# Batch 0's scores taken key tile by key tile over both kv pairs, with the value and sum matmuls of two query tiles split into single key tiles

## The chip, the cores and the metric

The kernel runs on one core of one Trainium2 chip. The metric is the device time of one execution in microseconds (us); the time before is the median of six runs. The engines are named as the profile names them: PE (TensorE, the matmul engine; PEld is its weight load), DVE (VectorE), ACT (ScalarE), POOL (GpSimd) and SP (SyncE, which here only issues DMAs).

## The reference

Grouped-query attention is followed by a gated MLP with a spatial gate, for eight batches:

```python
# attention: q (8, 16, 384, 64), k and v (8, 4, 384, 64); 4 query heads share one kv head
scores = matmul(q, k^T) / sqrt(64)
attn   = exp(scores - max) / sum(exp(scores - max))
x      = matmul(attn, v)                       # heads side by side: (8, 384, 1024)
# gated MLP
h      = relu(x @ w_in)                        # 1024 -> 1024
u, v   = h[..., :512], h[..., 512:]
v_n    = (v - mean(v)) / sqrt(var(v) + 1e-6)
v_s    = w_spatial @ v_n + b_spatial           # over the 384 positions
out    = (u * v_s) @ w_out                     # 512 -> 1024
```

## The kernel before, in words

**The work of one batch.** The 384 positions are three tiles of 128. A score unit is one query tile (`qt`), one pair of kv heads (`gp`, 0 or 1) and one key tile (`t`): `score_mm` (L363) makes a 128x1024 tile of scores with two matmuls that each use 64 rows of the PE array, and `exp` (L377) turns it into the fp16 tile `aT` on ACT. There are 18 units in a batch; the units go by query tile, then pair, then key tile. Two PSUM tiles hold scores (`ps_sc`, two buffers, L149), so a score unit can be computed when the exponential two units back is done.

`value_mm` (L388, matmuls on L395) multiplies `aT` with v, 32 columns at a time: `part` 0 and 1 are the two halves of the head dimension, `part` 2 multiplies with ones and so gives the sums of the softmax. One call is 12 matmuls over three key tiles and four kv heads, and it accumulates in one PSUM bank. The reciprocal of the sums comes from ACT as a logarithm and an exponential (`rec_ln`, `rec_exp`) or, for the first query tile of batch 0 alone, from DVE (`rec_v`, L414); `xmul` (L420) multiplies on DVE and leaves x transposed in `xt`.

The MLP follows: `v_mm` (steps V) or its halves (`v_part`, L595) for the v half of `h`, `relu`, `stats`, `rstd` and `norm` for `v_n`, `sp_part` for the spatial product (tile `psp`), `u_part` for the u half (`pu`), `sp_add` and `gate` on DVE, `o_part` for the output product (`po`), `o_copy` and `store`. The `..._part` functions use half of the array's rows and are paired, one on the low rows and one on the high rows. Between the two phases of such a pair stands a `mark` (L691): a tiny memset on DVE or POOL that waits for the end of phase 0 and that phase 1 waits for.

**What sets the order.** The order of every instruction on every engine is written out by hand in three plans, run by `run` (L729): `FIRST` for batches 0 to 2, `STEADY` once for each of batches 3 to 6, and `LAST` for batch 7. A step is a name, a batch (relative in `STEADY` and `LAST`) and arguments. The steps that matter here:

- `S`, `E`: the next score unit, the next exponential; `X,b,qt,part`: a value product; `rv`, `rl`, `re`: reciprocals; `xm`: `xmul`.
- `lk`, `lq`, `lv`, `lwi`, `lwo`, `lws`: loads of k, q, v, w_in, w_out, w_spatial. `lwi` goes out on POOL's queue and the first q tile of pair 0 on ACT's, all others on SP's.
- `ck`, `cq`, `cv`, `cws`, `cwo`: casts to fp16, with the engine as last letter (`v` DVE, `s` ACT, `p` POOL). `Tk`, `Tq`, `Tw`: transposes on PE; `tk`, `tq`, `tw`: the copies of their results. For batches from 2 on, `dk` and `dq` transpose by DMA instead.
- `V`, `ru`, `bs`, `rs`, `nm`: v half, relu, statistics, rstd, norm. `G`: a part of a paired product (`gs` spatial, `gu` u half, `go` output, `w..` v half beside output), `mk`: its mark.
- `W,0,n`: n warm-up matmuls of the identity with itself, whose result nobody reads.

Each engine runs its own steps in the order of the plan and waits only for its data and its buffers. Results other than scores go to four further PSUM banks, handed out in the order in which they were last read (`bank`, `read`, L168 and L174).

**The head of the kernel.** Before batch 0's first score, k and q are loaded, cast and transposed on PE. Batch 0's pair 0 is loaded first; the plan begins with 33 warm-up matmuls, then `Tk` and `Tq` of pair 0. Score units 0 to 2 need pair 0 alone, units 3 to 5 pair 1. The first `X` stands behind score unit 8.

Of the kernel before, what the change touches and what calls it, by code (L numbers as in the profile page):

```python
# [10 lines left out]
FP32 = mybir.dt.float32  # L11
# [7 lines left out]
SPLIT = 0  # L19

FIRST = """
lk,0,0,2 W,0,2 W,0,4 W,0,2 W,0,4 lq,0,0,0,1,0,1,s cq,0,0,0,1,1,0,1,p W,0,4 W,0,4 W,0,2 W,0,4 W,0,4
ck,0,0,0,3,s W,0,2 W,0,1 lq,0,1,0,1 cq,0,0,0,1,0,0,1,v Tk,0,0,0,3 Tq,0,0,0,0,1 lk,0,2,4
tq,0,0,0,0,1,v lq,0,0,1,3 tk,0,0,0,3,s lq,0,1,1,3 ck,0,1,0,3,p lk,1 lv,0 cq,0,1,0,1,1,0,1,p
cq,0,1,0,1,0,0,1,p lwi,0,1,2 lwi,0,1,1 lv,1 lwi,0,1,3 W,0,3 W,0,2 cq,0,1,1,3,1,0,1,p S,0 W,0,4 S,0
W,0,1 lq,1,0 Tk,0,1,0,3 Tq,0,1,0,0,1 S,0 W,0,1 E,0 lq,1,1 E,0 tk,0,1,0,3,v tq,0,1,0,0,1,v S,0 lws,0
lk,2 W,0,2 lwi,0,1,0 ck,1,0,0,3,p ck,1,1,0,3,p cv,0,p S,0 W,0,4 cq,0,0,1,3,0,0,1,v
cq,0,0,1,3,1,0,1,v lbi,0 lq,2,0 Tq,0,0,1,0,1 S,0 Tq,0,0,2,0,1 cq,1,0,0,1,0,0,1,p cq,0,1,1,3,0,0,1,v
tq,0,0,1,0,1,v S,0 Tq,0,1,1,0,1 W,0,1 Tq,0,1,2,0,1 E,0 lq,2,1 S,0 Tk,1,0,0,3 E,0 tq,0,0,2,0,1,v E,0
tk,1,0,0,3,v E,0 tq,0,1,1,0,1,v tq,0,1,2,0,1,v S,0 E,0 X,0,0,2 S,0 E,0 E,0 S,0 X,0,0,0 E,0 lwi,0,0,0  # L30
cq,1,1,0,1,0,0,1,p E,0 S,0 X,0,0,1 S,0 E,0 X,0,1,2 rv,0,0 xm,0,0,0 xm,0,0,1 lwi,0,0,3
cq,1,0,1,3,0,0,1,p S,0 X,0,1,1 X,0,1,0 cq,1,0,1,3,1,0,1,p E,0 S,0 rl,0,1 S,0 V,0,0,0,4 E,0 re,0,1
xm,0,1,1 V,0,0,4,8 S,0 xm,0,1,0 cv,1,v E,0 cws,0,0 lwi,0,0,1 cq,1,1,1,3,1,0,1,p cws,0,2 cws,0,1 E,0
lwi,0,0,2 cq,1,1,1,3,0,0,1,p S,0 cq,1,0,0,1,1,0,1,v ru,0,0,v V,0,1,0,4 Tq,1,0,0,0,1 Tk,1,1,0,3 E,0
E,0 tq,1,0,0,0,1,v bs,0,0 tk,1,1,0,3,s X,0,2,2 S,0 S,0 V,0,1,4,8 cq,1,1,0,1,1,0,1,v
cq,2,0,0,3,1,0,1,p cq,2,0,0,3,0,0,1,p Tq,1,1,0,0,1 tq,1,1,0,0,1,v rl,0,2 E,0 re,0,2 E,0 X,0,2,0
cq,2,1,0,3,0,0,1,p cq,2,1,0,3,1,0,1,p X,0,2,1 S,0 S,0 xm,0,2,0 xm,0,2,1 ru,0,1,v Tq,1,0,1,0,1
V,0,2,0,4 Tq,1,0,2,0,1 Tw,0,2,3 S,0 E,0 tq,1,0,2,0,1,v S,0 E,0 tw,0,2,3 bs,0,1 tq,1,0,1,0,1,v
ck,2,1,0,3,v ck,2,0,0,3,s E,0 V,0,2,4,8 Tw,0,0,2 Tq,1,1,1,0,1 E,0 tq,1,1,1,0,1,s ru,0,2,v tw,0,0,2
bs,0,2 X,1,0,2 S,0 rl,1,0 X,1,0,0 X,1,0,1 Tq,1,1,2,0,1 S,0 re,1,0 xm,1,0,0 S,0 E,0 xm,1,0,1 rs,0  # L40
dk,2 lwo,0,0 E,0 nm,0,2 nm,0,1 tq,1,1,2,0,1,v dq,2,0 lwo,0,1 nm,0,0 E,0 dq,2,1 lwo,0,2 lwo,0,3
V,1,0,0,4 V,1,0,4,8 S,0 ru,1,0,v G,0,gs,2,0,0,1 S,0 mk,0,gs,2,v E,0 G,0,gs,0,0,0,1 G,0,gs,2,1,0,1
S,0 mk,0,gs,0,v E,0 G,0,gs,0,1,0,1 E,0 S,0 sa,0,2 sa,0,3 sa,0,1 sa,0,0 X,1,1,2 E,0 rl,1,1 lk,3
X,1,1,0 X,1,1,1 lv,2 lq,3,0 lq,3,1 S,0 re,1,1 G,0,gu,2,0,0 S,0 G,0,gu,2,0,1 E,0 S,0 xm,1,1,1
xm,1,1,0 G,0,gu,0,0,0 E,0 E,0 cwo,0,0,1,v cwo,0,1,1,v S,0 G,0,gu,0,0,1 cwo,0,0,0,p mk,0,gu,2,p S,0
G,0,gu,2,1,0 mk,0,gu,0,p S,0 G,0,gu,0,1,0 E,0 G,0,gu,0,1,1 S,0 G,0,gu,2,1,1 gt,0,0 gt,0,3 gt,0,2 E,0
S,0 X,1,2,1 X,1,2,2 E,0 cwo,0,1,0,p E,0 S,0 cwo,0,2,1,v gt,0,1 cwo,0,2,0,v S,0 V,1,1,0,4 V,1,1,4,8
cwo,0,3,1,p E,0 rl,1,2 E,0 E,0 cwo,0,3,0,s re,1,2 G,0,go,0,0,0 ru,1,1,v S,0 xm,1,2,1 S,0 E,0
G,0,go,0,0,1 E,0 X,1,2,0 mk,0,go,0,p G,0,go,0,1,0 xm,1,2,0 bs,1,0 ck,3,0,0,3,v S,0 E,0 G,0,go,0,1,1
oc,0,0,v cv,2,p cq,3,0,0,3,1,0,1,p ck,3,1,0,3,p oc,0,1,s cq,3,0,0,3,0,0,1,v S,0 cq,3,1,0,3,0,0,1,p  # L50
cq,3,1,0,3,1,0,1,p X,2,0,2 X,2,0,0 S,0 rl,2,0 E,0 G,1,w12,2,0,0 G,1,w12,2,0,1 E,0 re,2,0 S,0 S,0
mk,1,w12,2,v bs,1,1 xm,2,0,0 G,1,w12,2,1,0 E,0 oc,0,2,v E,0 G,1,w12,2,1,1 S,0 ru,1,2,s oc,0,3,s
X,2,1,2 bs,1,2 X,2,0,1 rl,2,1 X,2,1,1 X,2,1,0 S,0 xm,2,0,1 re,2,1 xm,2,1,1 E,0 rs,1 G,2,w24,0,0,0
S,0 nm,1,0 xm,2,1,0 nm,1,2 G,2,w24,0,0,1 S,0 E,0 mk,2,w24,0,v nm,1,1 G,2,w24,0,1,0 S,0 E,0 oc,0,4,v
E,0 G,2,w24,0,1,1 E,0 ru,2,0,s lq,4,0 dk,3 lv,3 dq,3,0 dq,3,1 G,1,gs,0,0,0,1 S,0 oc,0,5,v
mk,1,gs,0,v S,0 G,1,gs,0,1,0,1 sa,1,0 E,0 G,1,gs,2,0,0,1 mk,1,gs,2,v sa,1,1 S,0 G,1,gs,2,1,0,1
G,1,gu,0,0,0 sa,1,3 sa,1,2 S,0 G,1,gu,0,0,1 mk,1,gu,0,v E,0 S,0 G,1,gu,2,0,0 G,1,gu,2,0,1
G,1,gu,0,1,0 S,0 E,0 E,0 mk,1,gu,2,v G,1,gu,0,1,1 S,0 G,1,gu,2,1,0 gt,1,0 S,0 G,1,gu,2,1,1 X,2,2,2
E,0 gt,1,1 bs,2,0 E,0 X,2,2,0 S,0 E,0 E,0 rl,2,2 re,2,2 E,0 gt,1,3 gt,1,2 G,2,w10,1,0,0
G,2,w10,1,0,1 mk,2,w10,1,v xm,2,2,0 S,0 S,0 G,2,w10,1,1,0 E,0 G,2,w10,1,1,1 E,0 S,0 st,0,1 lv,4 lk,4  # L60
X,2,2,1 oc,1,0,v oc,1,1,v ru,2,1,s bs,2,1 xm,2,2,1 cv,3,p st,0,2 lq,4,1 st,0,0 st,1,0 E,0
"""

STEADY = """
ck,1,0,0,3,p ck,1,1,0,3,p X,0,0,2 rl,0,0 X,0,0,0 S,0 G,-1,w12,2,0,0 G,-1,w12,2,0,1 re,0,0 S,0 S,0
E,0 E,0 cv,1,p cq,1,0,0,3,1,0,1,p cq,1,1,0,3,1,0,1,p cq,1,0,0,3,0,0,1,p xm,0,0,0 mk,-1,w12,2,v
cq,1,1,0,3,0,0,1,s G,-1,w12,2,1,0 G,-1,w12,2,1,1 oc,-2,3,s dq,1,0 oc,-2,2,s dk,1 S,0 lv,2 st,-2,1
dq,1,1 lk,2 ru,-1,2,v X,0,1,2 lq,2,1 lq,2,0 X,0,0,1 X,0,1,0 X,0,1,1 bs,-1,2 xm,0,0,1 rl,0,1 re,0,1
rs,-1 E,0 E,0 xm,0,1,0 G,0,w24,0,0,0 G,0,w24,0,0,1 nm,-1,1 nm,-1,0 xm,0,1,1 mk,0,w24,0,v nm,-1,2 S,0
S,0 E,0 G,0,w24,0,1,0 E,0 oc,-2,4,v G,0,w24,0,1,1 S,0 G,-1,gs,0,0,0,1 mk,-1,gs,0,p ru,0,0,s  # L70
oc,-2,5,v S,0 G,-1,gs,2,0,0,1 G,-1,gs,0,1,0,1 mk,-1,gs,2,p E,0 S,0 G,-1,gs,2,1,0,1 sa,-1,0 sa,-1,1
sa,-1,3 sa,-1,2 X,0,2,2 E,0 rl,0,2 X,0,2,0 X,0,2,1 re,0,2 E,0 S,0 G,-1,gu,0,0,0 G,-1,gu,0,0,1
mk,-1,gu,0,p xm,0,2,1 xm,0,2,0 E,0 G,-1,gu,2,0,0 S,0 G,-1,gu,0,1,0 G,-1,gu,2,0,1 S,0 S,0
G,-1,gu,0,1,1 mk,-1,gu,2,p G,-1,gu,2,1,0 E,0 E,0 G,-1,gu,2,1,1 E,0 S,0 gt,-1,0 gt,-1,1 gt,-1,2
gt,-1,3 S,0 G,0,w10,1,0,0 bs,0,0 G,0,w10,1,0,1 E,0 S,0 S,0 E,0 E,0 mk,0,w10,1,v E,0 G,0,w10,1,1,0
G,0,w10,1,1,1 S,0 ru,0,1,s oc,-1,0,v oc,-1,1,v st,-1,0 st,-2,2 bs,0,1 E,0
"""

LAST = """
S,0 X,0,0,2 G,-1,w12,2,0,0 G,-1,w12,2,0,1 E,0 rl,0,0 S,0 S,0 mk,-1,w12,2,v G,-1,w12,2,1,0  # L80
G,-1,w12,2,1,1 ru,-1,2,v oc,-2,3,v S,0 X,0,1,2 X,0,0,1 re,0,0 E,0 oc,-2,2,s rl,0,1 bs,-1,2 X,0,0,0
xm,0,0,1 xm,0,0,0 X,0,1,1 X,0,1,0 S,0 re,0,1 E,0 E,0 rs,-1 E,0 xm,0,1,1 G,0,w24,0,0,0 nm,-1,2
G,0,w24,0,0,1 mk,0,w24,0,v nm,-1,0 xm,0,1,0 S,0 S,0 G,0,w24,0,1,0 oc,-2,4,v G,0,w24,0,1,1 ru,0,0,v
E,0 E,0 X,0,2,2 oc,-2,5,s X,0,2,0 X,0,2,1 rl,0,2 V,0,1,0,4 bs,0,0 V,0,1,4,8 re,0,2 xm,0,2,1 nm,-1,1
ru,0,1,s xm,0,2,0 SP,-1,1 SP,-1,2 V,0,2,0,4 V,0,2,4,8 bs,0,1 sa,-1,1 U,-1,3 SP,-1,3 ru,0,2,v bs,0,2
sa,-1,2 rs,0 U,-1,1 SP,-1,0 U,0,0,1 nm,0,2 st,-2,1 sa,-1,3 U,-1,2 sa,-1,0 gt,-1,3 gt,-1,1 nm,0,1
U,-1,0 nm,0,0 st,-2,2 gt,-1,0 gt,-1,2 SP,0,1 SP,0,0 O,-1,0 sa,0,1 sa,0,0 oc,-1,0,v O,-1,5 SP,0,2
O,-1,3 O,-1,4 sa,0,2 oc,-1,4,s oc,-1,3,s oc,-1,5,s O,-1,1 SP,0,3 U,0,2 oc,-1,1,v gt,0,0 gt,0,2 U,0,1
gt,0,1 sa,0,3 O,-1,2 st,-1,2 U,0,3 gt,0,3 oc,-1,2,s O,0,1,0,3 O,0,4 O,0,1,3,4 O,0,0,0,3 oc,0,4,s
st,-1,0 st,-1,1 O,0,0,3,4 O,0,2 O,0,3 st,0,2,0,512 oc,0,0,v oc,0,1,s oc,0,2,v oc,0,3,s st,0,0  # L90
st,0,1,0,512 st,0,1,512,1024 lo,0,5
"""

# [2 lines left out]
def kernel(  # L96
# [20 lines left out]
    P = 128  # L117

    B, HQ, S, D = q.shape
# [5 lines left out]
    NST = S // P  # L125
# [234 lines left out]

    def score_mm(b, u, j0=0, js=1):  # L363
        qt, gp, t = u // 6, (u % 6) // 3, u % 3
        sc = ps_sc.tile([P, 2, 512], FP32, name=f"sc_{b}_{u}_{j0}", tag="sc")
        for half in range(2):
            lo, hi = half * D, (half + 1) * D
            nc.tensor.matmul(  # L368
                sc[:, half, 0 : 512 // js],
                kT[b][lo:hi, gp, t, :],  # L370
                qT[b, gp][lo:hi, qt, j0::js],
                start=True,
                stop=True,
            )
        held["sc", b, u, j0] = sc

    def exp(b, u, j0=0, js=1):  # L377
        qt, gp, t = u // 6, (u % 6) // 3, u % 3
        if (b, qt) not in aT:
            aT[b, qt] = att_a.tile([P, NGP, NST, 2, 512], FP16, name=f"aT_{b}_{qt}", tag="aT")  # L380
        nc.scalar.activation(  # L381
# [3 lines left out]
            scale=scale,  # L385
        )

    def value_mm(b, qt, part):  # L388

        a = aT[b, qt]  # L390
        v16 = loaded["v16", b]
        dst = bank([P, 512], FP32, f"X_{b}_{qt}_{part}")
        for t in range(NST):
            for g in range(HKV):
                nc.tensor.matmul(  # L395
                    dst[32 * g : 32 * (g + 1), :],
# [2 lines left out]
                    start=(t == 0),  # L399
                    stop=(t == NST - 1),  # L400
                )
        held["X", b, qt, part] = dst

    def rec_ln(b, qt):
        r = r_pool.tile([P, 512], FP32, name=f"rec_{b}_{qt}", tag="rec")
# [370 lines left out]
```

## Time and profile before

| | |
|---|---|
| median of six runs | 248.7 us (248.16 to 249.32) |
| the profiled execution, its own time | 249.3 us |
| its span, first to last instruction | 247.5 us |
| mean granted PE clock over the span | 0.997 |
| PE busy | 239.2 us, 97% |
| ACT busy | 190.7 us, 77% (139.9 us in exponentials) |
| DVE busy | 143.8 us, 58% |
| POOL busy | 42.8 us, 17% |

The profile shows one execution. "Busy" is the time in which at least one instruction of the engine runs; matmuls are pipelined, so that a busy PE says little by itself, and the distance from one matmul's start to the next is the better measure. In a line of the timeline the first two numbers are the start of a group of like instructions and the time from there to the end of the last one, both in us; a bracket at the end gives the idle time before and what ended it. A line of windows gives, for a stretch of time, each engine's busy time and its number of instructions.

### The profile page before, as it was taken

The page shows a single profiled execution, that of the slowest core. Times are in us where ns is not written, and L with a number is a line of the kernel's source. Part 1 is how long each engine was busy: PE and PEld are TensorE (multiplying, and loading weights), DVE is VectorE, ACT ScalarE, POOL GpSimd, SP SyncE. Part 2 cuts the span into 40 slices and gives each one's busy share as a digit, 9 for nine tenths or more (in the row PEclk, how much of TensorE's full clock was granted, in tenths as well). Part 3 has the DMA queues.
Part 4 walks back from the last instruction along what each step waited for, and adds up shares of the span by engine and source line. Part 5 has one row for each costly group of instructions (what it writes and reads, how often), then busy time and mean ns, then how long its engine had stood idle before and what let it go on. Part 6 is the DMA issues. An engine that isn't in the chain of part 4 may idle for free.

```text
span 247.5 us, 6053 instructions
## 1 busy us (share of the span) xinstructions
PE 239.2 (97%) x2556; PEld 120.5 (49%) x2556; DVE 143.8 (58%) x280; ACT 190.7 (77%) x249; POOL 42.8 (17%) x87
## 2 busy tenths in 40 slices
PE   7899998999999999999999999999999999999993
PEld 7434444543448444554445544554445544455551
DVE  0476698456774558636476447636476437777532
ACT  3899898999987888878997899888997797610221
POOL 1811914205015100033000600024000000000000
PEclk9999999999999999999999999999999999999998
DMA  7999999995999079910999049930950042200156
GB/s 175 293 219 343 245 216 196 273 320 162 263 322 276 3 172 199 300 45 12 260 243 285 4 171 223 299 108 3 265 151 0 3 165 91 85 2 1 41 223 247
DMA packets 57756, 42.73 MB, mean 173 GB/s; under 512 B 26881, under 2 KB 53889, under 8 KB 57729
## 3 DMA queue, kind: packets, MB, share of 16 engines
q1 hardware_dynamic: 54368, 39.85, 57.8%
q0 software_dynamic: 2176, 2.10, 5.6%
q10 hardware_dynamic: 1184, 0.39, 0.6%
q8 instruction: 20, 0.33, 0.5%
q14 instruction: 8, 0.06, 0.1%
HBM read 25.95 MB, written 12.58 MB: 156 GB/s over the span
## 4 chain that ended last, share of the span: by engine, by line
PE 84%; ACT 10%; DVE 3%; issue 1%; POOL 0%; POOLq 0%
PE X L395 18%; PE pu L613 13%; PE sc L368 11%; PE po L640 11%; PE pv L600 11%; ACT aT L381 7%; PE psp L626 4%; PE po L545 4%; PE pv L438 4%; PE pu L510 4%; PE warm L705 2%; DVE v_n L470 2%; PE psp L484 2%; DVE v_s L496 1%; ACT rec L412 1%
## 5 line engine op out<-in xcount | busy, mean ns | idle before, releaser
L381 ACT ACTIVATE aT<-sc 128x1024 f16<-128x1024 f32 x144 | 139.9, 1025 | 17.7 <-PE sc L368 17.7
L640 PE MATMUL po<-w_out,gT 64*128 64x512 f16 x288 | 66.9, 376 | 0.4 <-DVE mark_v L694 0.4
L600 PE MATMUL pv<-w_in,xt 64*128 64x512 f16 x272 | 64.5, 376 | 0.0
L368 PE MATMUL sc<-qT,kT 64*128 64x512 f16 x288 | 50.5, 380 | 1.3 <-ACT aT L381 1.3
L424 DVE TENSOR_TENSOR xt<-X,rec 128x512 f16<-128x512 f32 x48 | 32.0, 685 | 13.0 <-ACT rec L412 7.7
L395 PE MATMUL X<-aT,v 128*32 128x512 f16 x576 | 35.8, 380 | 0.0
L613 PE MATMUL pu<-xt,w_in 64*128 64x384 f16 x384 | 35.6, 322 | 0.0
L640 PEld LDWEIGHTS <-gT 64*128 64x128 f16 x288 | 25.7, 94 | 16.5 <-DVE mark_v L694 3.0
L600 PEld LDWEIGHTS <-xt 64*128 64x128 f16 x272 | 25.1, 94 | 15.9 <-issue 2.1
L522 DVE SCALAR_TENSOR_TENSOR gT<-pu,v_s 128x384 f16<-128x384 f32 x31 | 16.0, 552 | 22.7 <-PE pu L613 18.9
L328 DVE COPY osb<-po 128x512 f32<-128x512 f32 x28 | 19.3, 690 | 15.4 <-PE po L640 9.2
L368 PEld LDWEIGHTS <-kT 64*128 64x128 f16 x288 | 15.9, 94 | 23.1 <-issue 11.9
L613 PEld LDWEIGHTS <-w_in 64*128 64x128 f16 x384 | 20.5, 94 | 11.8
L328 POOL CAST q<-q 128x768 f16<-128x768 f32 (+2 forms) x29 | 21.0, 751 | 25.7 <-DMA q<-in_q_dram 20.5
L326 ACT ACTIVATE osb<-po 128x512 f32<-128x512 f32 x19 | 10.6, 595 | 18.1 <-PE po L545 17.4
L496 DVE TENSOR_TENSOR v_s<-psp,bias_b 128x384 f32<-128x384 f32 x32 | 20.3, 684 | 6.9 <-PE psp L626 6.3
L395 PEld LDWEIGHTS <-v 128*32 128x32 f16 x576 | 16.4, 96 | 14.4 <-issue 2.1
L395 PE MATMUL X<-aT,ones 128*32 128x512 f16 x288 | 20.1, 382 | 0.2
L696 POOL MEMSET mark_p<- 1x1 f32 x19 | 1.9, 102 | 104.8 <-PE psp L626 70.7
L406 ACT ACTIVATE rec<-X 128x512 f32<-128x512 f32 x23 | 13.8, 600 | 6.5 <-PE X L395 6.2
L459 DVE BATCH_NORM_STATS2 stats<-v_r 128x6 f32<-128x512 f32 x24 | 16.6, 690 | 3.0 <-issue 1.4
L449 DVE TENSOR_SCALAR v_r<-pv 128x512 f32<-128x512 f32 x12 | 8.2, 687 | 13.2 <-PE pv L600 10.7
(59 smaller groups left out, 204.3 us busy)
## 6 DMA issues: line engine op xcount, KB each, us to landing
out_dram<-osb SPq DMA_DIRECT2D x22, 512.0 KB, 3.7
q<-in_q_dram SPq DMA_DIRECT2D x14, 768.0 KB, 7.8
v<-in_v_dram SPq DMA_DIRECT2D x8, 384.0 KB, 4.9
k<-in_k_dram SPq DMA_DIRECT2D x7, 384.0 KB, 4.4
w_in<-in_moe_w_in_dram POOLq DMA_DIRECT2D x8, 256.0 KB, 7.4
w<-in_moe_w_out_dram SPq DMA_DIRECT2D x4, 512.0 KB, 4.5
q<-in_q_dram SPq DMA_DIRECT2D x2, 512.0 KB, 6.5
out_dram<-osb SPq DMA_DIRECT2D x3, 256.0 KB, 2.4
```

The source lines that it names most:

```text
L328: engine.tensor_copy(dst, src)
L368: nc.tensor.matmul(sc[:, half, 0 : 512 // js], kT[b][lo:hi, gp, t, :], qT[b, gp][lo:hi, qt, j0::js], start=True, stop=True,)
L381: nc.scalar.activation(aT[b, qt][:, gp, t].rearrange("p h (j q) -> p h j q", j=G)[:, :, j0::js], held["sc", b, u, j0][:, :, 0 : 512 // js] ...
L395: nc.tensor.matmul(dst[32 * g : 32 * (g + 1), :], v16[:, g, t, 32 * part : 32 * (part + 1)] if part < 2 else ones32, a[:, g // 2, t, g % 2 ...
L406: nc.scalar.activation(r, held["X", b, qt, 2], AF.Ln)
L424: nc.vector.tensor_tensor(xt[:, jj, :, qt * P : (qt + 1) * P], held["X", b, qt, jj].rearrange("p (j q) -> p j q", j=G), held["rec", b, qt] ...
L459: nc.vector.bn_stats(s6, held["v_r", b, st])
L496: nc.vector.tensor_tensor(held["v_s", b][:, m, :].rearrange("p (t s) -> p t s", t=NST), held["psp", b, m][:, 0:S].rearrange("p (t s) -> p ...
L522: nc.vector.scalar_tensor_tensor(held["gT", b][:, mu, :], held["pu", b, mu][:, 0:S], 0.0, held["v_s", b][:, mu, :], op0=ALU.max, op1=ALU.mult,
L600: yield lambda kc=kc: nc.tensor.matmul(held["pv", b, st], xT[b][rows, kc, st * P : (st + 1) * P], w_in16[rows, kc, DH:DFF], start=(first a ...
L613: yield lambda kc=kc: nc.tensor.matmul(held["pu", b, mu][:, 0:S], w_in16[rows, kc, mu * P : (mu + 1) * P], xT[b][rows, kc, :], start=(firs ...
L640: yield lambda m=m: nc.tensor.matmul(held["po", b, i], held["gT", b][rows, m, tt * P : (tt + 1) * P], w_out16[rows, m, half * 512 : (half ...
```

## The change

Two functions change, and all three plans are written anew.

In batch 0 the units go by query tile, then key tile, then pair: unit 1 is already pair 1. The other batches keep their order. `value_mm` takes a range of key tiles, so that a product can be made in pieces, with other work of PE between them:

```diff
+    def unit(b, u):
+        if b == 0:
+            return u // 6, u % 2, (u % 6) // 2
+        return u // 6, (u % 6) // 3, u % 3
...
-        qt, gp, t = u // 6, (u % 6) // 3, u % 3
+        qt, gp, t = unit(b, u)
...
-    def value_mm(b, qt, part):
+    def value_mm(b, qt, part, t0=0, t1=NST):
...
-        dst = bank([P, 512], FP32, f"X_{b}_{qt}_{part}")
-        for t in range(NST):
+        if t0 == 0:
+            held["X", b, qt, part] = bank([P, 512], FP32, f"X_{b}_{qt}_{part}")
+        dst = held["X", b, qt, part]
+        for t in range(t0, t1):
```

The plans, cut to PE's steps of the head (before, then after; the steps `W` ahead of the first `Tk` are 33 and 28 matmuls):

```diff
-Tk,0,0,0,3 Tq,0,0,0,0,1 W,0,3 W,0,2 S,0 W,0,4 S,0 W,0,1 Tk,0,1,0,3 Tq,0,1,0,0,1 S,0 W,0,1 S,0 W,0,2 S,0
-W,0,4 Tq,0,0,1,0,1 S,0 Tq,0,0,2,0,1 S,0 Tq,0,1,1,0,1 W,0,1 Tq,0,1,2,0,1 S,0 Tk,1,0,0,3 S,0 X,0,0,2 S,0 S,0
-X,0,0,0 S,0 X,0,0,1 S,0 X,0,1,2 S,0 X,0,1,1 X,0,1,0 S,0 S,0 V,0,0,0,4 V,0,0,4,8 S,0 S,0
+Tk,0,0,0,3 W,0,2 W,0,4 W,0,4 Tq,0,0,0,0,1 W,0,1 Tk,0,1,0,3 W,0,2 S,0 Tq,0,1,0,0,1 S,0 S,0 W,0,4
+Tq,0,0,2,0,1 S,0 S,0 Tq,0,0,1,0,1 W,0,2 X,0,0,2,0,1 S,0 X,0,0,2,1,2 Tq,0,1,1,0,1 S,0 X,0,0,1,0,1
+X,0,0,2,2,3 S,0 X,0,0,0,0,1 S,0 W,0,4 X,0,0,1,1,2 S,0 X,0,0,0,1,2 X,0,0,1,2,3 S,0 X,0,0,0,2,3 Tk,1,0,0,3
+S,0 Tk,1,1,0,3 Tq,0,1,2,0,1 S,0 X,0,1,1,0,1 X,0,1,1,1,2 X,0,1,0,0,1 S,0 X,0,1,2,0,1 X,0,1,0,1,2
+X,0,1,2,1,2 X,0,1,2,2,3 X,0,1,1,2,3 X,0,1,0,2,3 S,0 S,0 V,0,0,0,4 S,0 V,0,0,4,8 Tq,1,0,0,0,1 S,0
```

Query tiles 0 and 1 of batch 0 have their value products split; query tile 2 and all other batches keep whole ones. The number of warm-up matmuls in all (51), of score units and of all other PE instructions is the same before and after (2556 matmuls).

The rest of what moves, engine by engine:

- **Loads on SP.** Before: k pair 0, q pair 1 (its first query tile), k pair 1, then the rest of q, k of batch 1, v of batch 0, v of batch 1, q of batch 1. After: k pair 0, k pair 1, q pair 1, the rest of q, v of batch 0, k and q of batch 1, w_spatial, v of batch 1; the first two tiles of w_out are asked for earlier, the first one ahead of k and q of batch 2.
- **Casts at the start.** ACT casts half of pair 0's q, pair 1's k and half of pair 1's q, all ahead of its first exponential (before: pair 0's k, and a copy of its transpose). DVE casts pair 0's k and the other half of its q, POOL the other half of pair 1's q.
- **Batch 1's second product, around 65 to 75 us.** The mark of `w24` stood on DVE behind three `xmul`s and two of the three `norm`s; now it stands behind the same `xmul`s and one `norm`. On ACT an exponential stood between `re` and `rs`; now `rs` follows at once. The score units that stood singly between the halves of `w24` now stand in twos between its phases.
- **STEADY.** The marks of the spatial product and one of the two of the u half go from POOL to DVE; one relu goes from DVE to ACT and one from ACT to DVE; one of ACT's two output copies goes to DVE; ACT casts another half of q; loads and casts are in another order. PE keeps three blocks of whole value products in each pass.
- **LAST.** The spatial and u products of batch 6 and the norms of batch 7 are in another order; the last steps are the same kinds, and the plan ends with the same split output product (`lo`).

## The prediction

> **What bounds the kernel now.** I read the busy time by stages first, then PE, ACT and DVE in order of time. The stages:
>
> ```profile
> 6.40:14.00 7.60, 6.66 (x62) 3.68 (x63) 3.17 (x9) 6.91 (x8) 6.36 (x11) 1.00 1.17 274
> 14.00:20.50 6.50, 6.14 (x86) 1.98 (x85) 5.13 (x5) 6.50 (x9) 0.00 (x0) 1.00 1.17 255
> 20.50:39.50 19.00, 18.22 (x174) 8.12 (x172) 15.30 (x30) 17.45 (x25) 9.36 (x15) 1.00 1.04 251
> 39.50:100.40 60.90, 60.40 (x700) 29.90 (x702) 36.20 (x75) 54.59 (x71) 12.36 (x20) 1.00 0.84 219
> 100.40:212.00 111.60, 111.36 (x1308) 55.82 (x1306) 63.22 (x124) 94.66 (x123) 13.54 (x34) 1.00 0.51 144
> ```
>
> After the stretch and its length stand busy times and counts of PE, PEld, DVE, ACT and POOL. From 39.5 us on PE is never idle for long (60.40 of 60.90, 111.36 of 111.60), and ACT has room. Up to 20.5 us it is ACT that has none: 6.91 of 7.60 and 6.50 of 6.50. So the kernel is two problems: a head paced by exponentials, then PE's work end to end. As PE's work is the same before and after (2556 matmuls, 51 of them warm-ups), only three things count: when PE reaches the end of the head, what it waits for later, and the tail.
>
> ACT in the head:
>
> ```profile
> 7.09 7.44 ACT L381 ACTIVATE aT<-sc 128x1024 f16<-128x1024 f32 x8 [1.17 <-PE sc L368]
> 13.43 5.68 ACT L381 ACTIVATE aT<-sc 128x1024 f16<-128x1024 f32 x6
> 19.01 0.59 ACT L406 ACTIVATE rec<-X 128x512 f32<-128x512 f32 x1
> 20.91 1.95 ACT L381 ACTIVATE aT<-sc 128x1024 f16<-128x1024 f32 x2
> 23.28 1.94 ACT L381 ACTIVATE aT<-sc 128x1024 f16<-128x1024 f32 x2 [0.41 <-PE sc L368]
> ```
>
> The eighth exponential starts at 13.43, the first at 7.09: one every 0.906 us. ACT's first idle time is the 0.41 us at 22.9. Until then no reordering of PE can bring anything that the exponentials don't allow; a late first exponential moves everything.
>
> **The start: later by 0.7 us.** Before, 33 warm-ups run from 1.37 to 4.86, 0.106 us each; the q transposes start at 5.32 and the first exponential 1.77 us later. Now 28 warm-ups, three k transposes and ten warm-ups stand ahead of the q transposes: 1.37 + 41 x 0.106 = 5.72, first exponential at 7.49 (+0.40). The second exponential needs pair 1, whose q is now the last of the four first loads. In the trace the last of these four is waited for until 6.51. From there: cast 0.52 (POOL's row for this shape), to 7.0; the first score at 6.85 and its change to a transpose 0.54, to 7.4; four transposes 0.39, copy 0.41, score 0.39, hand-overs: 8.7, against 7.09 + 0.906 = 8.00 before. The exponentials therefore run 0.7 us late. Where the cover goes: before, units 0 to 2 needed pair 0 alone and gave pair 1 until 8.95.
>
> **The split value products: nothing at the exponentials' pace.**
>
> ```profile
> 14.74 0.39 PE L368 MATMUL sc<-qT,kT 64*128 64x512 f16 x2
> 15.49 0.39 PE L368 MATMUL sc<-qT,kT 64*128 64x512 f16 x2 [0.36 <-ACT aT L381]
> 15.81 0.83 PE L395 MATMUL X<-aT,v 128*32 128x512 f16 x12
> 16.58 0.39 PE L368 MATMUL sc<-qT,kT 64*128 64x512 f16 x2
> 16.90 0.83 PE L395 MATMUL X<-aT,v 128*32 128x512 f16 x12
> ```
>
> A product and a score take 0.76 + 0.32 = 1.08 us here, more than an exponential, so PE falls behind from 15.8 on. The split lets PE begin the products some 3 us earlier, in time that it spent on warm-ups and waits. But counted by score unit it gains nothing: at unit 12 both plans have done three whole products, at unit 13 four products' worth, at unit 14 six. Going on at 0.906 us from 8.7, the twelfth exponential ends near 18.9; unit 13 follows, then six thirds at 0.22 us (12 matmuls followed by more of their kind take 0.66), unit 14 at 21.0 (20.48 before) and V at 21.6 (21.01 before). With rec, the remaining exponentials and the products of query tile 2 (3 x 0.66 + 0.1), unit 20 comes at 28.4, against 28.73; but half of V of position tile 1 (0.87 + 0.1) is still to do, so PE is 0.6 us behind.
>
> [...]
>
> **The end of the head: 0.6 us late shrinks to 0.25.** Here PE waits before:
>
> ```profile
> 36.52 2.08 DVE L470 TENSOR_SCALAR v_n<-v_r,mv,rstd 128x512 f16<-128x512 f32 x2
> 38.52 0.41 DVE L328 COPY qT<-pq 128x512 f16<-128x512 f16 x1
> 38.85 0.53 DVE L470 TENSOR_SCALAR v_n<-v_r,mv,rstd 128x512 f16<-128x512 f32 x1
> ```
>
> PE's last score ahead of the spatial product starts at 38.27; the product starts at 39.44, after 0.78 us of waiting for the third v_n. The first two v_n took 1.04 each beside POOL's casts of batch 2's q (36.53 to 38.32), the third 0.53. In the new order this chain is: V of tile 2 ends near 33.6, relu 0.6, sums and their rec by 36.3, an exponential (its spacing 0.9), rstd 0.45, two xmul 1.3, three v_n at 0.53 and one qT copy 0.4: 39.65; PE is ready at 39.6. Spatial product 0.25 us later than before. From both sides: 0.85 earlier, if PE is late for nothing and v_n is there (38.6); 1.2 later, if all three v_n take 1.04 or w_spatial's casts, now behind more casts on POOL, hold back the transposes.
>
> **The middle: 0.6 us less.** The longest PE wait after the head:
>
> ```profile
> 69.55 1.00 DVE L470 TENSOR_SCALAR v_n<-v_r,mv,rstd 128x512 f16<-128x512 f32 x2
> 70.02 0.06 DVE L694 MEMSET mark_v<- 1x1 f32 x1
> ```
> ```profile
> 69.33 0.38 PE L368 MATMUL sc<-qT,kT 64*128 64x512 f16 x2
> 70.15 0.39 PE L640 MATMUL po<-w_out,gT 64*128 64x512 f16 x1 [0.45 <-DVE mark_v L694]
> ```
>
> A score unit between halves costs 0.22 us; this one takes 0.82, since the mark is behind two v_n. With one v_n (0.53) and one exponential (0.9) fewer ahead of it, the mark comes over a microsecond earlier: the whole 0.6 goes. What is late next is the end of phase 0 itself. Lower end nothing, upper end 0.8 with the small waits at 72.6 to 74.5.
>
> **STEADY: +0.1 in all.** A pass takes 28.07 us (100.38 to 128.45), and PE waits almost nowhere. Three blocks of products stay three. Marks that go from POOL to DVE queue behind two output copies of 0.69 us; the second ends about when phase 0 of the spatial product does (score 0.22 + 0.49 + hand-over), so up to 0.15 us each pass, 0.6 in four. Against it the relus and copies swap at 0.60 to 0.69 each; loads, casts and DMA transposes are early by whole score units. Bounds -0.2 and +0.8. **Tail: 0.** From the last matmul's end, 243.4, to 247.5 the same copy and store; order ahead of it within 0.3 either way.
>
> **Sum:** 0.25 - 0.6 + 0.1 = -0.25 us on a span of 247.5. The profiled execution took 249.3, 0.6 above the median of the runs; the same step from the median 248.7 gives 248.4. All lower bounds: -0.85 - 0.8 - 0.2 - 0.3 = -2.15, 246.5; all upper: 1.2 + 0 + 0.8 + 0.3 = +2.3, 251.0.
>
> **Rivals.** *PE ahead (247.2).* The reciprocal of query tile 0, 3.36 us on DVE, starts earlier than at 14.87, and batch 1's q is no longer asked for behind v, which held SP's queue from 7.46 to 14.15. If transposes and v_n are then always in time, PE's 0.85 before the spatial product goes too: -0.85 - 0.6 = -1.45. Against: ACT without a gap to 22.9.
>
> *The late start is paid in full (250.0).* Everything up to unit 17 hangs on the second exponential; 0.41 us of ACT's time is spare at 22.9 and 0.78 of PE's at 38.6, and what lateness exceeds these goes to the end one for one. With the three casts ahead of ACT's first exponential and pair 1's q landing 1.2 us later than 6.5 (as the rest of q does, waited for until 10.1, if loads crowd each other), the second exponential is at 9.9, 1.9 late, and 1.3 stays. It decides from a second exponential at about 9.4. For: loads share one stream (274 GB/s in that stage); against: the bytes of the first four loads are the same.
>
> *It doesn't do what it says (248.7).* The accumulation between scores only fills PE's waiting, nothing else moves, and the marks cancel.
>
> **Chances.** Forecast (0.8 us either way) 0.40, PE ahead 0.30, late start 0.22, nothing 0.08. This kernel's runs can tell about 0.3%, 0.75 us. Faster: 0.28 of PE ahead, 0.10 of the forecast: 0.38. Slower: 0.20 of the late start, 0.05 of the forecast: 0.25. Within: 0.37. The range 246.9 to 250.3 holds both rivals and cuts 0.4 and 0.7 from the bounds, where every unknown would have to fall to one side; the forecast's own is 247.6 to 249.2.
>
> **What would show it.** Right: second exponential near 8.7; V at 21.6; no wait of PE at the mark near 70; passes of 28.1 us. Wrong: a second exponential at 8.0 (then 0.7 better), one past 9.4, gaps of ACT between exponentials before 20 us, PE waiting for transposes of batch 1 or w_spatial near 29, or DVE's marks showing as PE waits in every pass.

## The result, and the profile after

The changed kernel takes 249.2 us in the median (248.36 to 250.61), the kernel before 248.4 us in the same comparison (247.45 to 249.32). The ratio is 1.0032, with a 95% interval of 1.0023 to 1.0040: slower by 0.8 us. The forecast was 248.4, 0.3 us below its base. The time lies in the range given, but it moved to the other side.

In the first two profiles the head is not where it was lost. ACT's first exponentials after (start, length, then the idle time before and what ended it):

```profile
6.85 1.01 ACT L389 ACTIVATE aT<-sc 128x1024 f16<-128x1024 f32 x1
8.41 6.52 ACT L389 ACTIVATE aT<-sc 128x1024 f16<-128x1024 f32 x7 [0.56 <-PE sc L376]
```

The second exponential is at 8.41, as the forecast had it in kind (8.7). But V starts at 21.09, against 21.01 before, and the spatial product at 38.40, against 39.44. (The profile before is of an execution of 249.3 us, the longest of its 68. In before_late, experiment 12 below, which has the same instructions up to there, V stands at 20.51 and the product at 38.04. So this pair alone does not settle the head; the part on the prediction comes back to it.) PE before at the spatial product, then PE after, around that product and at the output product some 15 us later:

```profile
39.44 0.66 PE L626 MATMUL psp<-wsT,v_n 64*128 64x384 f16 x6 [0.78 <-DVE v_n L470]
```
```profile
38.40 0.65 PE L635 MATMUL psp<-wsT,v_n 64*128 64x384 f16 x6
...
40.78 0.38 PE L376 MATMUL sc<-qT,kT 64*128 64x512 f16 x2
41.91 0.83 PE L405 MATMUL X<-aT,ones 128*32 128x512 f16 x12 [0.75 <-DVE v_s L505]
```
```profile
55.67 0.38 PE L649 MATMUL po<-w_out,gT 64*128 64x512 f16 x2
56.63 0.39 PE L649 MATMUL po<-w_out,gT 64*128 64x512 f16 x2 [0.58 <-POOL w_out L330]
```

No wait for `v_n` is left at 38.40. In its place PE waits twice where it did not before: 0.75 us at 41, for a bank that the addition of the bias (`v_s`) must read first, and 0.58 us at 56, in the middle of a product's half, for POOL's cast of the last tile of w_out. The mark's wait at 70 went, as forecast: in the profile after, two score units start at 70.09 behind a half, and the next half follows 0.47 later; a score unit costs 0.22.

Both new waits end in a load. SP's queue, before and then after (start and length of issuing; w_out's tiles land 4.0 to 4.7 us after the issue before and 4.7 to 13.2 after):

```profile
27.09 4.60 SPq L218 DMA_DIRECT2D q<-in_q_dram  x2
...
39.37 1.03 SPq L256 DMA_DIRECT2D w<-in_moe_w_out_dram  x1
...
43.12 0.75 SPq L256 DMA_DIRECT2D w<-in_moe_w_out_dram  x1
...
46.37 2.76 SPq L256 DMA_DIRECT2D w<-in_moe_w_out_dram  x2
```
```profile
29.64 0.37 SPq L220 DMA_DIRECT2D q<-in_q_dram  x1
30.06 0.57 SPq L271 DMA_DIRECT2D bias_b<-in_moe_b_spatial_dram  x1
...
46.54 0.83 SPq L258 DMA_DIRECT2D w<-in_moe_w_out_dram  x1
47.46 1.44 SPq L319 DMA_TRANSPOSE qT<-q  x1
50.60 0.33 SPq L258 DMA_DIRECT2D w<-in_moe_w_out_dram  x1
```

Before, the bias was asked for at 20.56 and all four tiles of w_out by 49.1. After, the bias stands behind batch 2's q, whose buffer waits for POOL's last cast of batch 1's q (28.99 to 29.6), and the last tile of w_out goes out at 50.60 (48.80 before), since its buffer waits for DVE's cast of the second tile. While SP stood still, little was in flight. The windows from 28 to 32 us, before and after; the last two columns are the DMA engines' share and GB/s:

```profile
28.00:32.00 4.00, 4.00 (x42) 1.85 (x38) 3.09 (x6) 3.48 (x5) 3.29 (x6) 1.00 1.02 226
```
```profile
28.00:32.00 4.00, 4.00 (x35) 2.24 (x33) 3.34 (x7) 3.74 (x6) 2.69 (x5) 1.00 0.59 80
```

226 GB/s became 80. Batch 2's q lands at 40.7 (POOL's cast of it starts there after 10.06 us of idling; before at 36.53), and the transposes by DMA of batch 2's k and q, on SP from 38 to 46 us before, stand there from 43 to 49 us, beside the loads of the last two tiles of w_out.

**Theory:** the loads that the new plan puts later (the bias, the last tiles of w_out, and batch 2's q with its transposes) cost the time; the new order of the units and the split do not. **Rivals:** the split with its changes of form on PE (a product takes 0.76 us ahead of a score, 0.66 ahead of another product) costs it; the later start of the exponentials costs it; the two profiles differ only by the luck of one execution.

### The profile page after: what moved, and what is told of

It is laid out like the page before. It is cut to its first block, busy times and chain, and to the rows that moved or that the text cites. A ratio compares the mean times of both kernels' runs of the same rounds, so it can differ in the third digit from the quotient of the medians.

```text
span 247.3 us, 6060 instructions
## 1 busy us (share of the span) xinstructions
PE 238.6 (96%) x2556; PEld 116.5 (47%) x2556; DVE 144.9 (59%) x295; ACT 186.7 (76%) x242; POOL 43.8 (18%) x79
## 4 chain that ended last, share of the span: by engine, by line
PE 91%; DMA 4%; DVE 1%; ACT 1%; POOL 1%; issue 1%; SPq 0%
PE X L405 20%; PE sc L376 14%; PE pu L622 12%; PE po L649 12%; PE pv L609 12%; PE psp L635 5%; PE pv L447 4%; PE po L554 4%; PE pu L519 4%; DMA w<-in_moe_w_out_dram 2%; DMA q<-in_q_dram 2%; PE psp L493 2%; PE pq L351 1%; ACT aT L389 1%; PE sc_u L519 1%
## 5 line engine op out<-in xcount | busy, mean ns | idle before, releaser
L405 PE MATMUL X<-aT,v 128*32 128x512 f16 x576 | 36.8, 380 | 0.0
L330 DVE COPY osb<-po 128x512 f32<-128x512 f32 x34 | 23.4, 691 | 20.4 <-PE po L649 13.2
L649 PEld LDWEIGHTS <-gT 64*128 64x128 f16 x288 | 26.3, 94 | 15.9 <-DVE mark_v L703 2.4
L609 PEld LDWEIGHTS <-xt 64*128 64x128 f16 x272 | 25.6, 94 | 14.5 <-issue 0.2
L330 POOL CAST q<-q 128x768 f16<-128x768 f32 (+2 forms) x29 | 21.6, 755 | 27.4 <-DMA q<-in_q_dram 26.4
L622 PEld LDWEIGHTS <-w_in 64*128 64x128 f16 x384 | 18.5, 94 | 14.7 <-issue 1.7
L405 PEld LDWEIGHTS <-v 128*32 128x32 f16 x576 | 15.2, 96 | 16.2 <-issue 2.1
L328 ACT ACTIVATE osb<-po 128x512 f32<-128x512 f32 x13 | 7.5, 597 | 18.8 <-PE po L554 17.9
L405 PE MATMUL X<-aT,ones 128*32 128x512 f16 x288 | 20.6, 382 | 0.7 <-DVE v_s L505 0.7
L705 POOL MEMSET mark_p<- 1x1 f32 x7 | 0.6, 88 | 103.3 <-PE pu L622 103.3
L421 ACT ACTIVATE rec<-rec 128x512 f32<-128x512 f32 x23 | 14.5, 629 | 0.4
```

Source lines behind the costliest of these rows:

```text
L330: engine.tensor_copy(dst, src)
L405: nc.tensor.matmul(dst[32 * g : 32 * (g + 1), :], v16[:, g, t, 32 * part : 32 * (part + 1)] if part < 2 else ones32, a[:, g // 2, t, g % 2 ...
L421: nc.scalar.activation(r, r, AF.Exp, scale=-1.0)
L609: yield lambda kc=kc: nc.tensor.matmul(held["pv", b, st], xT[b][rows, kc, st * P : (st + 1) * P], w_in16[rows, kc, DH:DFF], start=(first a ...
L622: yield lambda kc=kc: nc.tensor.matmul(held["pu", b, mu][:, 0:S], w_in16[rows, kc, mu * P : (mu + 1) * P], xT[b][rows, kc, :], start=(firs ...
L649: yield lambda m=m: nc.tensor.matmul(held["po", b, i], held["gT", b][rows, m, tt * P : (tt + 1) * P], w_out16[rows, m, half * 512 : (half ...
```

## The experiments

Each kernel is compared with the kernel before on the same chip. The profiles show one execution each.

**1. The changed kernel again.**

> The changed kernel once more, unaltered, beside the kernel before, as the base of what follows. All theories expect 1.002 to 1.004 of the kernel before. If the two profiles differed only by when PE reached full speed at the start, this second profile shows neither of the two new waits of PE (0.8 us at 40.8, in front of the u half; 0.6 us at 55.7, in front of the output product); if the waits belong to the new order of the queues, it shows both again, each within 0.3 us of the first profile.

249.3 us, ratio 1.0036 (1.0015 to 1.0056). The waits are there again, but divided differently: the one for the bias is 0.19 us, the one at 56 is gone, and a new one stands at 54. PE, then ACT:

```profile
52.33 0.59 PE L649 MATMUL po<-w_out,gT 64*128 64x512 f16 x4
54.37 0.39 PE L376 MATMUL sc<-qT,kT 64*128 64x512 f16 x2 [1.45 <-ACT aT L389]
```
```profile
52.78 0.63 ACT L328 ACTIVATE w_out<-w 128x512 f16<-128x512 f32 x1 [2.48 <-DMA w<-in_moe_w_out_dram]
```

ACT's idle time gives the cause: it waits 2.48 us for the third tile of w_out, and the exponential that frees the score's bank is queued behind that cast. The tile was asked for at 46.13 and took 6.6 us; in the first profile, asked for at 46.54, ACT had it at 51.28. Batch 2's second q transpose, issued at 47.05, took 7.0 us as well (5.3 at most in the first profile), so that the score could not have run before 54.05 in any case. Which load is late, and by how much, changes from one execution to the other; that PE waits over 1.3 us in all for loads between 40 and 62 us does not, in these two. The expectation that each wait comes back within 0.3 us failed.

**2 to 4. One or two loads moved.**

```diff
@@ after_bias
-... lws,0 lv,1 lwo,0,0 lk,2 ... lq,2,0 lbi,0 lq,2,1
+... lws,0 lbi,0 lv,1 lwo,0,0 lk,2 ... lq,2,0 lq,2,1
@@ after_wout
-cwo,0,1,0,p mk,0,gu,2,p ... cq,3,1,0,3,0,0,1,p cwo,0,1,1,v
+cwo,0,1,0,p cwo,0,1,1,v mk,0,gu,2,p ... cq,3,1,0,3,0,0,1,p
```

> One step is moved: the load of the spatial bias goes out on SP right behind w_spatial's instead of behind the first q tile of batch 2, where it waited for POOL's casts of batch 1's q. Theory of the queues: the first addition of the bias on DVE no longer waits for the load, PE's wait at 40.8 goes, and the time falls by 0.7 to 0.9 us, to 0.999 to 1.001 of the kernel before. Rival, the split itself and its changes of tile form cost the time: no change, 1.002 to 1.004. Rival, the wait is hidden by a later one: the wait goes from the profile, the psp of batch 1 starts as late as before the move, and the time stays.

> One step is moved: DVE's cast of half of the second w_out tile comes ahead of the marks and gates of batch 0, so that its buffer is free earlier and the load of the last w_out tile goes out about 3 us earlier. Theory of the queues: PE's wait at 55.7 for the last tile of w_out goes, and the time falls by 0.5 to 0.6 us, to about 1.001 of the kernel before. Rival, split: no change, 1.002 to 1.004. Risk: the cast of about 0.5 us on DVE now stands ahead of other DVE work at 45 to 50 us and shifts marks or gates.

> Both moves together. Theory of the queues: the gains add up, 1.2 to 1.5 us less than the changed kernel, 0.996 to 0.999 of the kernel before, which would show that the new unit order and the split cost nothing by themselves. Rival, split: no change, 1.002 to 1.004. Rival, hidden: less than the sum of the two single moves, since one wait absorbs part of the other.

| | median | ratio |
|---|---|---|
| after_bias | 249.3 us | 1.0029 (1.0014 to 1.0044) |
| after_wout | 249.2 us | 1.0030 (1.0018 to 1.0043) |
| after_bias_wout | 249.6 us | 1.0043 (1.0022 to 1.0065) |

None of them is faster than the changed kernel. By time alone the rival "split" would have won here. The traces say otherwise. With the bias early, its wait is gone, but PE waits 1.38 us for the score at 54.29, and batch 1's spatial product starts at 72.95, against 72.50 and 73.47 in the changed kernel's two profiles. The profile names an exponential of ACT, which was done at 52.9; what fits is batch 2's second q transpose, issued at 47.38 and landed 6.9 us later. With only the cast moved, the bias landed 12.4 us after its issue. DVE in that kernel:

```profile
42.61 2.53 DVE L505 TENSOR_TENSOR v_s<-psp,bias_b 128x384 f32<-128x384 f32 x4 [2.62 <-DMA bias_b<-in_moe_b_spatial_dram]
```

With both, the last tile is asked for 1.9 us earlier (48.73 against 50.60), and yet POOL's cast of it starts at 55.09 instead of 55.42: PE waits for it as before (0.5 us). The issue 1.9 us earlier brought 0.33 us. So in the profiles of after_bias and after_wout the single wait taken away was taken up by another load, which is the third theory in the expectation of after_bias. For both moves together no profile shows it: that of after_bias_wout has 0.53 us as its longest wait and is of an execution of 248.8 us, 0.8 below its median, so what its median is made of stays open.

**5. The kernel before again.**

> The kernel before once more, unaltered, against itself: 1.000 within 0.001 of the other runs of it, and a second profile, as the first was of its slowest execution. If the loads decide, the stretch from 40 to 62 us has again under 0.4 us in single waits of PE, in contrast to the changed kernel, whose waits there summed to over 1.5 us in each of four profiles of it and its one-step variants.

248.7 us, ratio 1.0009 (0.9992 to 1.0025). No single wait of PE stands between 40 and 62 us in its second profile either; the two old ones are there (0.46 us for `v_n` at 39.13, 0.4 us at the mark near 70). The waits on loads belong to the new plan, not to the luck of one execution.

**6 and 7. All w_out loads and the bias early.** SP's queue gets the bias and the second tile ahead of batch 2's q (w_out_hole); then POOL also casts the first two tiles in its idle stretch, so that the other two can go out at once (w_out_early):

```diff
@@ w_out_hole and w_out_early
-lk,2 ... lq,2,0 lbi,0 lq,2,1 ... lwo,0,1
+lk,2 lwo,0,1 lbi,0 ... lq,2,0 lq,2,1
@@ w_out_early
+cwo,0,0,0,p cwo,0,0,1,p lwo,0,2 cwo,0,1,0,p cwo,0,1,1,p lwo,0,3 cq,2,0,0,3,1,0,1,p
-cq,2,0,0,3,0,0,1,p cwo,0,0,0,p ck,2,1,0,3,p ... lwo,0,2 ... lwo,0,3 ... cwo,0,0,1,p ... cwo,0,1,0,p ... cwo,0,1,1,v
```

> SP's queue alone is altered: the second w_out tile and the bias go out ahead of batch 2's q, which waits for POOL's casts in any case, into the stretch from 28 to 32 us in which the DMA engines moved 80 GB/s only. Nothing else moves; the last two w_out tiles stay where they are. Theory, late w_out loads: the bias wait at 41 goes, but the waits for the last two w_out tiles at 51 to 56 stay, so the time falls by 0.3 us at most, 1.001 to 1.004 of the kernel before. Rival, the split itself: no change.

249.1 us, 1.0026 (1.0007 to 1.0045). As expected the bias wait went and the time stayed. But the wait that stayed is for the transposed q, which took 6.9 us to land, more than for w_out. PE in this kernel:

```profile
54.61 0.39 PE L376 MATMUL sc<-qT,kT 64*128 64x512 f16 x2 [1.42 <-DMA qT<-q]
```

The theory "late w_out loads" is thereby too narrow: w_out's tiles and the transposes are in flight together and are late in turns.

> As the one before, and the first two w_out tiles are cast on POOL in its idle stretch from 31 to 40 us, so that the loads of the last two can go out there, ahead of the transposes of batch 2 by DMA, instead of at 46.5 and 50.6. One of the four casts goes from DVE to POOL by this. Theory, late w_out loads: PE's waits between 40 and 62 us go, 1.5 to 2.0 us, and the time falls to 0.992 to 0.998 of the kernel before, faster than it. Rival, the split itself or the new unit order cost the time: 1.002 to 1.004 stays. Risk: batch 2's q lands later because more is loaded beside it.

248.2 us, 0.9991 (0.9974 to 1.0009). The interval lies wholly below that of the changed kernel (1.0023 to 1.0040): 1.0 us came back, without a touch to the order of the units or the split. Its spatial product starts at 38.52, as in the changed kernel (38.40 and 38.62); from there to the end it takes 207.8 us, against 208.9 and 209.7. The expectation also wanted it to be faster than the kernel before; that can't be told. SP and PE in this kernel:

```profile
32.00 5.07 SPq L258 DMA_DIRECT2D w<-in_moe_w_out_dram  x2
```
```profile
48.97 0.39 PE L376 MATMUL sc<-qT,kT 64*128 64x512 f16 x2 [0.50 <-ACT aT L389]
...
55.46 0.59 PE L649 MATMUL po<-w_out,gT 64*128 64x512 f16 x4
```

The last two tiles go out at 32.00 and 36.09 and land by 45.9, and the output product runs through: four matmuls in a row at 55.46, where the changed kernel broke after two. One wait is left, 0.50 us at 48.97, for the first of batch 2's transposed q. The two transposes of q land 4.0 to 4.5 us after their issue here, against 3.8 to 7.0 in the changed kernel and the variants that left the last two tiles where they were.

**8. The split alone.** As w_out_early, with the value products of query tiles 0 and 1 whole, each at the place of its last piece:

```diff
-X,0,0,2,0,1 S,0 ... X,0,0,2,1,2 ... X,0,0,2,2,3 S,0
+S,0 ... X,0,0,2 S,0
```

> As the one before, with the value products of batch 0's first two query tiles whole again, each at the place of its last piece, in the new order of the units. Theory, late w_out loads, with the split worth nothing at the exponentials' pace: the same time as the one before within 0.3 us. If the split pays, this is slower by about what the pieces gained, 0.5 to 1.5 us; if the split's changes of tile form cost, it is faster by up to 0.2 us.

248.5 us, 1.0013 (0.9996 to 1.0030): 0.3 us above w_out_early in the median, which the intervals cannot tell from nothing. The traces can tell more. First the start of V in w_out_early, then in this kernel:

```profile
20.98 1.04 PE L447 MATMUL pv<-w_in,xt 128*128 128x512 f16 x4
```
```profile
21.94 1.04 PE L447 MATMUL pv<-w_in,xt 128*128 128x512 f16 x4
```

The second exponentials are 0.01 us apart (8.30 and 8.29), so 0.96 us at V is what the split gains over whole products at these places. Other places may cost less: from the second exponential to V it is 12.68 us in w_out_early and 13.65 here, but 13.00 in the kernel before, with whole products in the old order of the units. At the spatial product 0.72 is left (38.52 and 39.24). The split pays in the head; its changes of form, of which the rival made a cost, do not show as one. The 0.3 us in the median can't be put down to it alone: in early_whole's profile PE also waits 0.89 us at 50.08 for a transposed q that took 5.7 us to land, with w_out's loads as early as in w_out_early.

**9 to 11. Batch 2's q earlier, and the old order of the units.**

```diff
@@ early_q, from w_out_early
-lwi,0,0,3 cq,1,0,1,3,0,0,1,p
+lwi,0,0,3 cq,1,0,1,3,0,0,1,v
@@ early_old_order, from w_out_early
-        if b == 0:
-            return u // 6, u % 2, (u % 6) // 2
-S,0 Tq,0,1,0,0,1 ... S,0 cq,0,0,1,3,1,0,1,v
+S,0 S,0 Tq,0,1,0,0,1 ... cq,0,0,1,3,1,0,1,v
```

The third kernel, early_q_old_order, has both edits.

> The kernel with early w_out loads, and one cast of batch 1's q moved from POOL (at 29.1, behind w_spatial's casts and a w_in load) to DVE (at about 26.5), so that batch 2's first q load goes out on SP at about 27 instead of 29.75 us. Theory, late loads: q lands some 2 us earlier, POOL's cast of it starts before 39.5 instead of at 40.9, the wait of 0.66 us at 47.7 for batch 2's transposed q goes, and the time falls by 0.4 to 0.7 us to 0.995 to 0.998 of the kernel before. Rival: loads in flight at 27 to 40 share one stream, so that q lands as late as before the move and nothing changes. Risk: DVE's cast pushes batch 0's relu and the first statistics 0.5 us later, which can make PE wait for the norms at 38.

> The kernel with early w_out loads, with the old order of batch 0's units (query tile, pair, key tile), the split of the value products kept; the second score stands ahead of pair 1's q transposes, and the second and third exponentials need pair 0 alone. It undoes the late start: the second exponential should come at about 7.8 instead of 8.4. Theory that the exponentials pace the head: 0.3 to 0.6 us less than the kernel with early w_out loads, unless PE then waits for the same loads. Rival, the order of the units is worth something by itself, as each query tile's key tile is done for both pairs one unit earlier: the same or slower.

> Both edits: the early q load and the old order of the units, on top of the early w_out loads. If the two gains are independent, 0.7 to 1.2 us less than the kernel with early w_out loads: 0.994 to 0.997 of the kernel before, the fastest here. If loads set the end of the head whatever PE does, no more than the early q load alone.

| | median | ratio |
|---|---|---|
| early_q | 248.5 us | 1.0002 (0.9990 to 1.0015) |
| early_old_order | 248.1 us | 0.9994 (0.9974 to 1.0014) |
| early_q_old_order | 248.3 us | 0.9990 (0.9980 to 1.0001) |

The one moved cast does what it was made for: POOL in early_q casts batch 2's q 4 us earlier (36.51 instead of 40.87), and the wait at 48.97 is gone. The time does not follow: the casts now run beside the norms (36.51 to 38.60; the spatial product starts at 38.49), PE waits 0.22 us for w_spatial's transposes in the middle of the spatial product, and the median lies 0.3 above w_out_early, again inside the intervals. In the old order the second exponential comes at 8.13 and 7.81, against 8.30 in w_out_early and 8.50 in early_q. The first ones differ too (7.21 and 6.89, against 6.75 and 7.26), as they do between two heads of the same instructions (last section), so no single pair gives the size of the late start. From the second exponential to V the two kernels with the old order take 13.23 and 13.24 us, the two with the new one 12.68. So on the way to V the new order wins about what its later second exponential loses (V at 21.36 and 21.05, against 20.98 and 21.18), and neither reached the time; the 0.994 to 0.997 expected of both edits were missed. None of the five kernels with early loads can be told from another or from the kernel before; the best by its interval, early_q_old_order, has 0.9990 with an upper end of 1.0001.

**12. The kernel before with one late load.** No new order and no split, only the last w_out tile behind k and v of batch 3:

```diff
-lwo,0,2 lwo,0,3 ... lv,2 lq,3,0
+lwo,0,2 ... lv,2 lwo,0,3 lq,3,0
```

> The kernel before, with one load moved on SP: the last w_out tile goes out behind k and v of batch 3 instead of ahead of them, some 1 to 2 us later, as late as in the changed kernel. Neither the new order nor the split is in it. Theory, late w_out loads: PE waits 0.3 to 1.0 us for that tile near 55 us and the time rises to 1.001 to 1.004 of the kernel before. Rival, the split or the order of the units cost the time: 1.000 within 0.001.

249.1 us, 1.0030 (1.0012 to 1.0049), as much as the whole change. PE, then ACT:

```profile
54.53 0.38 PE L640 MATMUL po<-w_out,gT 64*128 64x512 f16 x2
56.97 0.39 PE L640 MATMUL po<-w_out,gT 64*128 64x512 f16 x2 [2.06 <-ACT w_out L326]
```
```profile
56.29 0.63 ACT L326 ACTIVATE w_out<-w 128x512 f16<-128x512 f32 x1 [2.45 <-DMA w<-in_moe_w_out_dram]
```

The load went out at 49.30 instead of 48.80, half a microsecond later and not 1 to 2, but behind 768 KB of k and v instead of ahead of them: it took 7.0 us to land, at least 2.1 more than any tile in two profiles of the kernel before (4.0 to 4.9). By the same edit k and v go out 2.0 us earlier (k at 47.16 instead of 49.18), and the third tile, now beside them, took 6.4. The same break after two matmuls of the output product appears as in the changed kernel. In this execution (250.1 us) it costs 2.06 us, in the median about 0.6. One late load, with neither part of the change, makes a loss as large as the whole change's; and with the loads early, in w_out_early, the change makes none, though its second exponential is nearly as late (8.30 against 8.41). That shows from both sides that the loads cost the time. How the 0.8 us divide among bias, w_out and transposes is not settled: it differs in each execution, and the single moves could not take one away without another in its place.

## Why the prediction was wrong, point by point

**The bound: right.** PE's work is the same and it is hardly idle from the end of the head on (busy 60.52 of the 62.00 us to 100.4 and all of the 111.60 to 212 in the first profile after), so only waits count. The list of waits was what failed.

**The start: right in kind; the size depends on the execution.** The second exponential is at 8.41 for 8.7. That is 0.40 later than in the first profile before (8.01), not 0.7, but 0.92 later than in before_late (7.49). The rival "paid in full" named 9.4 as the point from which it decides, so by its own sign it is out; and w_out_early, which starts nearly as late (8.30), loses nothing that can be told.

**"The split value products: nothing at the exponentials' pace": wrong in part.** From the second exponential to V the change takes 12.68 us, the kernel before 13.00: 0.3 gained, and the split is worth more than that against whole products in the new order (early_whole). The forecast's V at 21.6 is also 0.4 later than its own terms give. From 18.9 the score of 0.32 and six thirds of 0.22 with 0.1 for the change of form (0.76 less 0.66) lead to unit 14 at 20.6, not 21.0; it was at 20.55, unit 13 at 18.82, V at 21.09. Against the first profile before V is 0.08 later, against before_late 0.58, where the forecast had 0.6. The 0.2 us expected at most of the changes of form is an estimate: two changes more in the head (26 against 24 among the first 150 matmuls of the two profiles) at this 0.1 us each. No run isolates it, and the split as a whole stands on the other side.

**The end of the head: open.** The forecast was 0.25 later. The spatial product starts at 38.40 and 38.62 in the two profiles after, at 39.44 and 39.13 in the two before: 0.5 to 1.0 earlier. But before_late has it at

```profile
38.04 0.66 PE L626 MATMUL psp<-wsT,v_n 64*128 64x384 f16 x6
```

without a wait for `v_n`, and against that the change is 0.4 to 0.6 later. So the 0.78 us of waiting that the forecast started from is not in every execution; before_again has 0.46. The two profiles before are of executions of 249.3 and 249.0 us, over the medians of 248.4 and 248.7. From the product to the end both take 208.1 us, and the time of an execution is 1.8 above its span; so an execution at the median of 248.4 would start the product near 38.5. By this estimate the head is about the same before and after.

What the profiles do show is the chain of `v_n`. The forecast counted it from a last reciprocal at 36.3, which made it 39.65. In the first profile after, that reciprocal ends at 35.0, the exponential behind it at 35.9, `rstd` at 36.3, and the three norms take 0.5 each; POOL's casts of batch 2's q, beside which two of them took 1.04 each in the first profile before, come 4 us later. This gain was named among the bounds (0.85 earlier) and in the rival "PE ahead". What was not seen is that the same lateness of q is part of the cost further on.

**The middle: right.** The mark's wait of 0.45 us is gone, and the two score units there take 0.47 us, 0.03 above twice 0.22.

**STEADY and the tail: right.** The spatial products of the passes in the first profile after start at 101.05, 129.10, 157.16 and 185.22, 28.05 or 28.06 us apart, against 28.07 before. No mark shows as a wait of PE. From the last matmul's end to the end of the span the kernel before takes 4.16 us, the changed one 3.99.

**The step that failed** is the sum's list of what PE "waits for later": it holds the wait that goes and no term for the loads that the change moves; what it says of loads behind the head, for the STEADY passes, is that they are early. The bias behind q on SP, and w_out's last tiles beside the transposes, stood in the plan, and no bounds were set for them. Measured: 0.2 to 2.1 us of PE for the bias, 0.5 to 1.5 for w_out and the transposed q, 1.3 and 1.6 together in the two profiles of the changed kernel. With the loads in time (w_out_early) the same change stands at 0.9991 of before (0.9974 to 1.0009). That this is near the 0.3 us of the forecast is luck: it can't be told from no change, and the terms of the head are not those that the forecast had.

The terms close on the profiles. From the start of the spatial product to the end, the kernel before takes 208.1 us (247.2 - 39.13), the changed one 208.9 (247.3 - 38.40): 0.8 longer. The waits give 0.75 + 0.58 - 0.45 (the mark's) = 0.9. In the second profile it is 209.7, 1.6 longer, and the waits give 0.19 + 1.45 + 0.21 (at 57.9, for an `xmul`) - 0.45 = 1.4.

The landing times are what a reader should have asked for. In the changed kernel and its one-step variants the late bias (192 KB) took 10.5 to 12.4 us from issue to landing, and the third tile (512 KB) 4.3 to 6.6. Here q, w_in and w_out were in flight beside the bias, and the same 192 KB took 8.7 us in the kernel before: what else was in flight fits as the reason, and no run isolates it.

## What to carry to other kernels

When a plan is reordered, list every load that changes its place, with its issue, its landing in the trace and its first reader; issued 0.5 us later but behind 768 KB, one tile cost 0.6 us here, in a kernel in which nothing else was altered. Compare the heads of two kernels in more than one profile each. If taking one such wait away changes nothing, look at whether the next load in the queue has taken it up before giving up the cause, and test it from the other side: make the same load late in the old kernel. A gain that comes from an engine's work being late (POOL's casts here, out of the norms' way) is to be followed to the reader of that work.

## What the runs showed of the hardware that was not expected

**The first exponential's time is partly luck.** The heads of the kernel before and of before_late are the same instructions, but in the profiles the first exponential starts at 7.09 and 6.57, and V at 21.01 and 20.51. PE's five warm-up matmuls between the q transposes and the first score, before and then in before_late:

```profile
5.72 0.74 PE L705 MATMUL warm<-ident 128*128 128x128 f16 x5
```
```profile
5.46 0.44 PE L705 MATMUL warm<-ident 128*128 128x128 f16 x5
```

0.107 us from start to start in the first, 0.056 in the second: PE doubled its speed at 7.3 us there and by 5.3 us here; in the first profile after it did so at 4.85. In the first profiles before and after that is 5.9 and 3.5 us after the first matmul, which starts at 1.37 in both; no run shows what sets the moment. The granted clock reads 1.00 in every window up to 12 us of these two and does not show it. The two heads of the same instructions are 0.50 us apart at V, so comparing the heads of two single profiles is good to half a microsecond at best.

**The releaser named is not always the one.** DVE's first addition of the bias, in the first and the second profile of the changed kernel:

```profile
41.19 2.53 DVE L505 TENSOR_TENSOR v_s<-psp,bias_b 128x384 f32<-128x384 f32 x4 [1.31 <-PE sc L376]
```
```profile
40.84 2.60 DVE L505 TENSOR_TENSOR v_s<-psp,bias_b 128x384 f32<-128x384 f32 x4 [0.75 <-DMA bias_b<-in_moe_b_spatial_dram]
```

It is the same wait. Where PE is named, the product that the addition reads had ended at 40.24; the score named is a later one, which ended at 41.16, and the bias landed at 41.09, 11.0 us after its issue. In the second profile of the kernel before, where the bias was asked for at 20.75, the first addition starts at 41.03, 0.04 us after its product's end.
